# Slot order for tokens of x, u and the output, stores in two halves, and a new order, in a gated-attention and token-mixing kernel

## The chip, the cores and the metric

The kernel runs on one core of a Trainium2 chip. The metric is the device time of one execution in microseconds. A core has five engines with a queue of their own: TensorE (PE, matmuls; its weight loads are listed as PEld), VectorE (DVE), ScalarE (ACT), GpSimd (POOL) and SyncE (SP, which here only issues transfers). Transfers between HBM and the on-chip memory run on 16 DMA engines; here SP and ACT issue them.

## The reference, cut to what matters

Four sequences of 768 tokens with 8 heads of 48 go through a linear attention with a decay per token and key dimension. The result, 384 wide, is x of a mixer: one pair of products over the tokens, one over the channels.

```python
for t in range(S):
    state = alpha[:, :, t, :, None] * state + np.einsum('bhd,bhe->bhde', k[:, :, t], v[:, :, t])
    y[:, :, t] = np.einsum('bhd,bhde->bhe', q[:, :, t], state)
...
h = np.maximum(xt @ w_tok1, 0.0) @ w_tok2      # over the 768 tokens, 256 wide
u = x + h.transpose(0, 2, 1)
h2 = np.maximum(u @ w_ch1, 0.0) @ w_ch2        # over the 384 channels, 1536 wide
return (u + h2)
```

All inputs and the output are float32. The kernel computes in bf16 with float32 sums.

## The kernel before, in words

**Chunks.** A batch of 768 tokens is cut into 3 chunks of 256, 12 chunks in all, called n = 0 to 11. A load brings one of alpha, k, q, v of a chunk as a tile of 128 partitions, 384 KB: partition p holds the tokens 2p and 2p + 1, its two *slots* (line 541, `load`). For chunk n the operations are: logarithms of alpha (`ln`, `lnP`), their running sum on PE (`cum`), its exponentials on ACT (`E`, `IE`), the products of k and q with them (`kk`, `kl`, `qq`, `ql`, line 653), a transposition of both, the products G of keys and queries (`G0_`, `G1_`, one for each half of 128 tokens), a mask (`mask0_`, `mask1_`, line 720, on DVE), the states K, `s`, `sa`, `sm`, the result `y`, and its copy to a tile of x (`x0_`, `x1_`, 128 tokens each).

**Transposition.** For the chunks 0 to 5 it runs on PE (`trk`, `trq`, line 666) and the result is copied from PSUM (`evk`, `evq`). For the chunks 6 to 11 it is a DMA transpose that SP issues (`dk`, `dq`, line 677), and the query gets one copy more (`pq`). The key's columns are in slot order after it. The query's copy (`qev`) also puts the two slots of each token next to each other, so that x, and with it u and the output, have their tokens in order on the partitions. For the chunks from 3 on, some halves of the keys are copied to the other partitions (`ka`, `kb`, `kc`); `kc` writes over the tile that `dk` reads, and so waits for it, and K waits for `kc`.

**Mixer.** For each batch b: `t1_b` (x by the first token weight, line 805), `ht`, `t2_b` (by the second, line 810), `u` (line 814), the transposition of u (on PE for the batches 0 and 1, `up` and `ut`; by DMA for 2 and 3, `ux`), `c1_b` (line 829, 24 groups of 3 matmuls), `rt` (the maximum with 0, on ACT line 800 or DVE line 802), `c2_b` (line 834), the output's addition `o` (line 838, DVE) and its store `st` (line 585). The last tile of the last batch is cut into 320 and 64 columns (`h0`, `h1`). There are four tiles for o and 20 load tiles. The weights come in 16 pieces of 384 KB (`ldw`) and are cast to bf16 (`cw`, line 698).

**Order.** Every operation, its engine and its place is written out in a list (`ORDER`: the last letter is the engine, t for PE, s for ACT, v for DVE, g for POOL, y for SP), with the buffer numbers of the tiles in another (`BUFS`). Engines take their operations strictly in that order. A planner made the lists beforehand; it is not part of the program. `f` are filler matmuls while PE waits. In the built program transfers take turns on eight semaphores, over both queues, so a transfer waits until the eighth before it has landed.

**Constants.** `mk` (the mask) is made by two fills and two selections on POOL (lines 512 to 516) and a copy on DVE (line 530).

Of the kernel before, what the change touches and what calls it, by code (L numbers as in the profile page):

```python
# [116 lines left out]
def build(g):  # L117
# [12 lines left out]
    def attention(n):  # L130
# [56 lines left out]
        if n < NX:  # L187
            bk, bq = V("one"), V("one")
            trk = O("trk", pe([128] * 8), 8, writes=[bk], reads=[pkk], preds=kk + fill("trk", bk),
                    emit=lambda e: g.trw(bk, pkk, True))  # L190
# [3 lines left out]
                    emit=lambda e: g.trw(bq, pkq, False))  # L194
            evq = O("evq", either(dve(1024 * 1.065), act(1024 * 1.34)), 9, writes=[tpq], reads=[bq], preds=[trq],
                    emit=lambda e: g.qev(e, tpq, g.bank(bq).bitcast(BF16)))
        else:
# [5 lines left out]
            evq = O("pq", either(dve(1024), act(1024 * 1.35, True), {"POOL": (1100.0, 1140.0)}), 9.5, port=True, writes=[tpq], reads=[tqx], preds=[xq],  # L203
# [72 lines left out]
    def weight(nm, piece, prio, work=1100.0):  # L276
        raw = V("in")
        o = P.op(f"ldw_{nm}{piece}", {"SP": (420.0, 420.0), "ACT": (374.0, 374.0)}, prio, writes=[raw],
                 emit=lambda e: g.weight(e, nm, piece, raw, o), dma=("i", work, 1500.0, 650.0))
        wl[(nm, piece)] = P.op(f"cw_{nm}{piece}", either(dve(768, True), pool_cp(768), act(768, True)), prio + 1,  # L280
                               reads=[raw], preds=[o], port=True, emit=lambda e: g.wcast(e, nm, piece, raw))

    def mixer(b):
# [56 lines left out]
        for i in range(NS):  # L340
            hold = 4000.0 if (i >= NS - 3 and b < B - 1) else 0.0
            cuts = [(0, 320), (320, HD)] if (b, i) == LAST else [(0, HD)]
            for ci, (ca, cz) in enumerate(cuts):
# [14 lines left out]
                P.op(f"st_{nm}", {"SP": (420.0, 420.0), "ACT": (374.0, 374.0)}, m0 + (16800 + 1950 * (i + 1)) * sc + hold,  # L358
                     reads=[o_], preds=[oo], emit=lambda e, i=i, o_=o_, ca=ca, cz=cz: g.store(e, o_, b, i, ca, cz),
                     dma=("o", OUT_NS * (cz - ca) / HD, 1000.0, 520.0))  # L360
# [15 lines left out]
f1_trq0t f3_cumw0t f3_trk0t ld_at0y ln0s f1_trq1t f3_trq0t ld_at1y ln1s cumw0t Et0s IE0s E0s f3_cumw1t cumw1t E1s  # L376
f3_K0t Et1s ld_kt0y kk0v f1_K0t ld_qt0y qq0v ql0v trq0t ld_vt0y ld_qt1y kl0v trk0t vb0v K0t evq0s IE1s evk0v G0_0t
vs1_0s ld_at2y ln2s s0_0v mask0_0v qq1g ql1g ib0t G1_0t sa1_0t f3_trq1t trq1t evq1s cumw2t E2s ld_kt1y kl1v IE2s
sm1_0v kk1g trk1t mask1_0v y1_0t x1_0s ld_vt1y Et2s vb1g K1t vs1_1g sa0_1t evk1v G0_1t ld_kt2y kk2v f1_G11t G1_1t kl2v
trk2t evk2s sm0_1v sa1_1t ld_qt2y ql2g ld_vt2y vb2s mask1_1v ib1t y1_1t x1_1s sm1_1v qq2g ia1t trq2t evq2s K2t sa0_2t  # L380
mask0_1v vs0_0g y0_0t x0_0v ld_at3y P3g lnP3s f3_G12t ln13s G0_2t ldw_wt10y cw_wt10g vs0_1g G1_2t t1_0_1_0t t1_0_1_1t
y0_1t x0_1s sm0_2v t1_0_0_0t mask0_2v cum3t E3s t1_0_0_1t t1_0_0_2t IE3s t1_0_1_2t ldw_wt11y cw_wt11g t1_0_0_3t ia2t
vs0_2g y0_2t x0_2s vs1_2g ib2t mask1_2v y1_2t x1_2s t1_0_1_3t t1_0_1_4t ld_kt3y kk3v k0a3v kl3v t1_0_0_4t ldw_wt21y
cw_wt21s t1_0_0_5t ht_0_0v t1_0_1_5t ht_0_1s ldw_wt20y cw_wt20g ka3g trk3t evk3v t2_0_3t u_0_3v t2_0_0t u_0_0v t2_0_2t
ld_at4y P4g t2_0_4t ln14s u_0_2v t2_0_1t u_0_1v lnP4s t2_0_5t u_0_5v up_0_1t ut_0_1s up_0_0t cum4t r13s E4s r14s kb3g
ldw_wc11y u_0_4v up_0_2t cw_wc11g ut_0_0v c1_0_2_0t rt_0_2_0s ldw_wc10y ld_vt3y ldw_wc13y IE4s cw_wc10v c1_0_0_0t
ut_0_2v c1_0_3_1t c1_0_1_1t kc3v vb3v c1_0_3_0t rt_0_3_1v ld_qt3y vs1_3v qq3v rt_0_1_1v q0r3v ql3v ldw_wc14y cw_wc13s
c1_0_7_0t c1_0_0_1t vs0_3s rt_0_3_0s rt_0_0_0s cw_wc14s c1_0_1_0t ldw_wc15y cw_wc15g rt_0_1_0v rt_0_7_0v K3t c1_0_6_1t
rt_0_0_1s trq3t rt_0_6_1v evq3s s0_3v c1_0_8_0t rt_0_8_0s sa1_3v ld_qt4y c1_0_8_1t rt_0_8_1v c1_0_7_1t rt_0_7_1s
c1_0_6_0t G1_3t mask1_3v G0_3t qq4g ldw_wc12y q0r4g ql4g c1_0_10_0t rt_0_10_0v c1_0_10_1t rt_0_10_1v c1_0_11_0t  # L390
cw_wc12s c1_0_4_1t trq4t c1_0_2_1t ld_kt4y rt_0_6_0v evq4s c1_0_5_0t mask0_3v c1_0_9_1t ldw_wc21y c1_0_5_1t c1_0_4_0t
cw_wc21s rt_0_4_0s rt_0_11_0v ib3t kk4g ld_qt5y k0a4g y1_3t kl4g kb4g rt_0_4_1v ld_at5y ln15s c1_0_11_1t rt_0_5_0v
ldw_wc20y c1_0_9_0t rt_0_9_1v trk4t rt_0_2_1s x1_3v y0_3t P5g lnP5s rt_0_11_1v rt_0_9_0s cw_wc20g c2_0_0_0t rt_0_5_1s
cum5t ldw_wc22y evk4v G0_4t ld_vt4y G1_4t mask1_4v sm1_3g x0_3s cw_wc22g c2_0_4_0t mask0_4v r15s q0r5g c2_0_0_1t
c2_0_4_1t vb4s vs1_4g vs0_4s ka4s kc4g E5s qq5v c2_0_1_0t ia4t ldw_wc23y cw_wc23s ldw_wc24y cw_wc24v c2_0_2_0t
c2_0_2_1t K4t sa0_4v IE5s c2_0_1_1t c2_0_1_2t c2_0_2_2t c2_0_4_2t ldw_wc25y y0_4t sm0_4v sa1_4v ld_at6y ib4t cw_wc25s
c2_0_1_3t P6v lnP6s y1_4t x1_4s trq5t ld_kt5y k0a5v kk5v c2_0_4_3t o_0_4v x0_4s ld_at7y sm1_4g ld_vt5y P7g ld_kt6y
cum6t evq5s trk5t evk5v ln16s c2_0_0_2t c2_0_0_3t vb5s vs0_5g vs1_5s ln17s r17s E6s o_0_1v G0_5t r16s mask0_5v G1_5t
mask1_5v c2_0_5_0t c2_0_5_1t c2_0_5_2t c2_0_5_3t ia5t y0_5t ld_at8y kc5g K5t P8v t1_1_1_0t t1_1_1_1t sa0_5v x0_5s
t1_1_1_2t t1_1_1_3t t1_1_1_4t c2_0_2_3t sm0_5v ib5t y1_5t o_0_5v x1_5s k0a6g t1_1_0_0t t1_1_0_1t IE6s kk6v t1_1_0_2t  # L400
kb6v t1_1_0_3t t1_1_0_4t ld_qt6y ld_qt7y t1_1_0_5t ht_1_0s t1_1_1_5t ht_1_1s c2_0_3_0t c2_0_3_1t t2_1_3t t2_1_1t
u_1_3v u_1_1v ld_vt6y t2_1_0t vb6s u_1_0v vs1_6g lnP7s st_0_5s lnP8s t2_1_2t ka6g u_1_2v cum7t t2_1_5t u_1_5v cum8t
st_0_1y E7s t2_1_4t u_1_4v c2_0_3_2t IE7s ld_at10y o_0_2v up_1_0t ut_1_0s ld_vt7y up_1_1t ut_1_1v ld_kt7y q0r6g
ld_at9y o_0_0v up_1_2t dk6y ut_1_2s qq6g dq6y vb7g c2_0_3_3t o_0_3v k0a7v kk7v IE8s vs0_6s E8s kc6s c1_1_2_0t
c1_1_6_0t rt_1_6_0s vs1_7s c1_1_11_1t c1_1_1_0t rt_1_1_0v q0r7g ld_qt8y c1_1_4_0t rt_1_11_1v ld_kt8y c1_1_8_0t
c1_1_5_0t dk7y c1_1_0_1t rt_1_4_0v rt_1_5_0s qq7v dq7y K6t rt_1_0_1s c1_1_0_0t c1_1_11_0t ln19s kb7s P9g ld_kt9y
rt_1_2_0v ka7s vs0_7g ln18s lnP9s rt_1_8_0s P10g lnP10s ld_vt8y c1_1_7_0t rt_1_0_0v c1_1_3_0t s0_6v sa1_6v rt_1_7_0v
sm1_6g k0a8v c1_1_6_1t c1_1_8_1t r18s q0r8v c1_1_10_0t c1_1_3_1t rt_1_11_0s kc7g c1_1_9_1t c1_1_4_1t rt_1_8_1v ld_qt9y
rt_1_10_0s rt_1_3_0s c1_1_7_1t rt_1_3_1s rt_1_7_1s K7t cum9t c1_1_1_1t rt_1_4_1s kk8v sa0_7v sm0_7v st_0_2s c1_1_9_0t
c2_1_1_0t st_0_4s IE9s rt_1_9_1s E9s rt_1_1_1s c1_1_2_1t ln110s r19s c1_1_5_1t sa1_7v pq6g G0_6t pq7s rt_1_6_1v  # L410
rt_1_9_0v dk8y qq8v dq8y st_0_0s G1_6t c2_1_1_1t c2_1_1_2t c1_1_10_1t c2_1_1_3t ld_qt10y rt_1_2_1s c2_1_4_0t rt_1_5_1v
# [12 lines left out]
rt_2_8_1s c1_2_0_0t c1_2_2_0t c1_2_9_1t rt_2_2_0v st_1_1s rt_2_0_1s rt_2_9_1s c1_2_1_0t K10t sa0_10v sm0_10v c2_2_5_0t
# [468 lines left out]
```

## Time and profile before

| | |
|---|---|
| time, median of 3 runs | 164.9 us (163.66 to 165.65) |
| time of the profiled execution | 164.64 us |
| its span | 162.9 us |
| PE busy | 154.4 us (95%) |
| DVE, ACT, POOL busy | 119.7, 94.8, 66.7 us |
| moved by DMA | 34.46 MB, of it 25.17 MB read from HBM and 4.72 MB written |
| granted PE clock | 1.00 until the end |

The span runs from the first to the last instruction; the time has some 1.7 us around it. A busy matmul counts until its modelled end, so in a row of matmuls of 326 ns each the next one starts 162 ns after the one before. In the rows, "ps" is PSUM, L834 is line 834, and what stands behind an arrow in brackets is what ended the idle time before the row.

### The profile page before, as it was taken

The page shows a single profiled execution, that of the slowest core. Times are in us where ns is not written, and L with a number is a line of the kernel's source. Part 1 is how long each engine was busy: PE and PEld are TensorE (multiplying, and loading weights), DVE is VectorE, ACT ScalarE, POOL GpSimd, SP SyncE. Part 2 cuts the span into 40 slices and gives each one's busy share as a digit, 9 for nine tenths or more (in the row PEclk, how much of TensorE's full clock was granted, in tenths as well). Part 3 has the DMA queues.
Part 4 walks back from the last instruction along what each step waited for, and adds up shares of the span by engine and source line. Part 5 has one row for each costly group of instructions (what it writes and reads, how often), then busy time and mean ns, then how long its engine had stood idle before and what let it go on. Part 6 is the DMA issues. An engine that isn't in the chain of part 4 may idle for free.

```text
span 162.9 us, 4036 instructions
## 1 busy us (share of the span) xinstructions
PE 154.4 (95%) x1598; PEld 97.8 (60%) x1598; DVE 119.7 (73%) x214; ACT 94.8 (58%) x178; POOL 66.7 (41%) x87
## 2 busy tenths in 40 slices
PE   7989798999999999989899999999999999999992
PEld 2556564566676766645567766666666656666661
DVE  4188988999979996996799888878788345442231
ACT  3878686796597787749996873248941211435000
POOL 4045694509982333938159999352130000000000
PEclk9999999999999999999999999999999999999998
DMA  5999999999899998999999999998511067200115
GB/s 130 325 325 322 281 352 347 315 329 336 278 346 269 274 324 203 320 121 269 242 277 175 239 258 187 165 275 233 117 48 50 2 129 209 97 4 0 48 60 181
DMA packets 76322, 34.46 MB, mean 212 GB/s; under 512 B 68112, under 2 KB 76304, under 8 KB 76304
## 3 DMA queue, kind: packets, MB, share of 16 engines
q1 hardware_dynamic: 74000, 31.10, 75.5%
q10 hardware_dynamic: 2304, 3.11, 5.2%
q8 instruction: 12, 0.20, 0.5%
q14 instruction: 6, 0.05, 0.1%
HBM read 25.17 MB, written 4.72 MB: 183 GB/s over the span
## 4 chain that ended last, share of the span: by engine, by line
PE 75%; DMA 12%; ACT 4%; DVE 2%; SPq 2%; issue 1%; POOL 1%; POOLq 0%; DVEq 0%; ACTq 0%
PE ps L834 29%; PE ps L829 24%; PE ps L604 13%; DMA tpk<-pkk 5%; DMA in<-in_moe_w_tok_dram 4%; PE ps L810 4%; PE ps L805 4%; DMA in<-in_alpha_dram 3%; SPq L545 2%; ACT rt L800 2%; PE ps L666 1%; DVE pkq L653 1%; POOL pkq L653 1%; DVE wc L698 1%; POOL wt L698 1%
## 5 line engine op out<-in xcount | busy, mean ns | idle before, releaser
L834 PE MATMUL ps<-wc,rt 128*128 128x384 bf16 (+2 forms) x300 | 52.9, 320 | 0.0
L829 PE MATMUL ps<-ut,wc 128*128 128x384 bf16 x288 | 50.2, 326 | 0.6 <-ACT rt L800 0.5
L829 PEld LDWEIGHTS <-wc 128*128 128x128 bf16 x288 | 27.3, 98 | 18.8 <-issue 0.9
L834 PEld LDWEIGHTS <-rt 128*128 128x128 bf16 x300 | 27.2, 98 | 16.4
L800 ACT ACTIVATE rt<-ps 128x384 bf16<-128x384 f32 x53 | 23.8, 490 | 19.9 <-PE ps L829 19.6
L720 DVE TENSOR_TENSOR gtm<-ps,mk 128x1024 bf16<-128x1024 f32 x24 | 28.7, 1218 | 3.0 <-PE ps L604 2.7
L802 DVE TENSOR_SCALAR rt<-ps 128x384 bf16<-128x384 f32 x43 | 22.5, 551 | 7.3 <-PE ps L829 7.2
L838 DVE TENSOR_TENSOR o<-ps,u 128x384 f32<-128x384 f32 (+2 forms) x25 | 13.2, 539 | 12.8 <-PE ps L834 9.6
L653 POOL TENSOR_TENSOR pkq<-in,E 128x384 bf16<-128x384 f32 (+1 forms) x9 | 11.4, 1272 | 9.3 <-DMA in<-in_q_dram 7.7
L814 DVE TENSOR_TENSOR u<-ps,x 128x384 bf16<-128x384 f32 x24 | 11.9, 550 | 3.4 <-PE ps L810 3.4
L653 DVE TENSOR_TENSOR pkk<-in,IE 128x384 bf16<-128x384 f32 (+1 forms) x11 | 7.6, 703 | 6.4 <-ACT IE L637 4.0
L697 ACT CAST x<-ps 128x384 bf16<-128x384 f32 x16 | 7.5, 481 | 7.3 <-PE ps L604 7.2
L698 POOL CAST vb<-in 64x384 bf16<-64x384 f32 (+1 forms) x17 | 9.4, 558 | 4.4 <-ACT vb L697 2.2
L805 PE MATMUL ps<-x,wt 128*128 128x384 bf16 x48 | 10.8, 325 | 0.0
L697 ACT CAST vb<-in 64x384 bf16<-64x384 f32 (+1 forms) x16 | 10.4, 653 | 0.3
L697 ACT COPY tpq<-ps 128x1024 bf16<-128x1024 bf16 x6 | 7.9, 1321 | 4.5 <-PE ps L666 4.5
L810 PE MATMUL ps<-ht,wt 128*128 128x384 bf16 x48 | 9.4, 326 | 0.5 <-POOL wt L698 0.5
L604 PE MATMUL ps<-zs 128*128 128x512 bf16 x25 | 8.3, 472 | 1.5 <-DVE zs L507 1.1
L604 PE MATMUL ps<-vb,gtm 128*128 128x48 bf16 x192 | 8.5, 183 | 0.7 <-DVE gtm L720 0.6
L653 POOL TENSOR_TENSOR pkk<-in,IE 128x384 bf16<-128x384 f32 (+1 forms) x6 | 8.5, 1409 | 1.4 <-DVE pkk L653 1.1
L604 PEld LDWEIGHTS <-gtm 128*128 128x128 bf16 x192 | 7.3, 96 | 2.2 <-DVE gtm L720 1.0
L604 PE MATMUL ps<-tpq,tpk 48*64 48x128 bf16 (+1 forms) x288 | 8.1, 219 | 0.6 <-ACT tpq L697 0.5
(93 smaller groups left out, 211.0 us busy)
## 6 DMA issues: line engine op xcount, KB each, us to landing
in<-in_alpha_dram SPq DMA_DIRECT2D x12, 384.0 KB, 5.6
in<-in_k_dram SPq DMA_DIRECT2D x12, 384.0 KB, 4.9
in<-in_q_dram SPq DMA_DIRECT2D x12, 384.0 KB, 5.2
in<-in_v_dram SPq DMA_DIRECT2D x12, 384.0 KB, 4.9
in<-in_moe_w_ch_dram SPq DMA_DIRECT2D x12, 384.0 KB, 6.3
out_dram<-o ACTq DMA_DIRECT2D x15, 192.0 KB, 1.9
in<-in_moe_w_tok_dram SPq DMA_DIRECT2D x4, 384.0 KB, 5.5
out_dram<-o SPq DMA_DIRECT2D x8, 192.0 KB, 2.7
```

The lines of the kernel that those rows point to most:

```text
L604: return self.pe.matmul(out, lhsT=lhsT, rhs=rhs, start=start, stop=stop, skip_group_check=True)
L653: self.shared(self.eng[e].tensor_tensor(self.t(dst)[:, c : c + z, :, 0:D], self.t(src)[:, :, c : c + z, :].rearrange("p h s d -> p s h d") ...
L697: return self.act.copy(d, s)
L698: return self.shared(self.eng[e].tensor_copy(d, s))
L720: self.nc.vector.tensor_tensor(self.t(gtm)[:, hf, :, :], self.pair(gp).rearrange("p a (j t) -> p (a j) t", t=128), bass.AP(tensor=m.tensor ...
L800: self.act.activation(d, s, AF.Relu)
L802: self.nc.vector.tensor_scalar_max(d, s, 0.0)
L805: self.pe.matmul(self.bank(bank)[:, 0:HD], lhsT=self.wt1[:, kc, m * 128 : m * 128 + 128], rhs=self.t(x), start=(kc == 0), stop=(kc == NS - 1))
L810: self.pe.matmul(self.bank(bank)[:, 0:HD], lhsT=self.wt2[:, kc, i * 128 : i * 128 + 128], rhs=self.t(hts[kc]), start=(kc == 0), stop=(kc = ...
L829: self.pe.matmul(self.bank(bank)[:, 0:HD], lhsT=self.wc1[:, kc, mc * 128 : mc * 128 + 128], rhs=self.t(ut)[:, 3 * half : 3 * half + 3, kc, ...
L834: self.pe.matmul(self.bank(bank)[:, 0 : cz - ca], lhsT=self.t(rts[mc][0])[:, i * 128 : i * 128 + 128], rhs=self.wc2[:, mc, ca:cz], start=( ...
L838: self.nc.vector.tensor_tensor(self.t(o)[:, ca:cz], self.bank(bank)[:, 0 : cz - ca], self.t(u)[:, i % 3, ca:cz], ALU.add)
```

## The change

Five things are changed.

1. Tokens of x, u and the output stay in slot order: partition 64 s + t of a tile holds token 2t + s of its 128. The copies of the query from PSUM (`evq`) are then plain copies, written like those of the key; the transposition of the query on PE writes the same layout as the key's. The copy `pq` moves runs of 64.
2. The rows of the first token weight are loaded in the same order: each of its two pieces comes in two transfers of 64 partitions (`ldw_wt10a`, `ldw_wt10b`, ...). The columns of the second are permuted in its cast, which reads its f32 tile with a step of two.
3. Each store becomes two: partitions 0 to 63 to the even rows, 64 to 127 to the odd rows (`st_...a`, `st_...b`). 25 stores become 50; 33 of them are issued by ACT (16 before), 17 by SP (9 before).
4. The mask is put together by four copies on DVE from `u2` and `us`, two constants that are there already; POOL's four operations for it go.
5. `ORDER` and `BUFS` are made anew: for all engines the operations stand in another order, and some are on another engine. For instance kc6 moves from ACT to POOL. The same 1,598 matmuls are issued.

```diff
@@ attention
-            evq = O("evq", either(dve(1024 * 1.065), act(1024 * 1.34)), 9, writes=[tpq], reads=[bq], preds=[trq],
-                    emit=lambda e: g.qev(e, tpq, g.bank(bq).bitcast(BF16)))
+            evq = O("evq", either(dve(1024, True), act(1024)), 9, writes=[tpq], reads=[bq], preds=[trq],
+                    emit=lambda e: g.trwev(e, tpq, bq))
@@ mixer
-                P.op(f"st_{nm}", {"SP": (420.0, 420.0), "ACT": (374.0, 374.0)}, m0 + (16800 + 1950 * (i + 1)) * sc + hold,
...
+                for slot in range(2):
+                    P.op(f"st_{nm}" + "ab"[slot], {"SP": (420.0, 420.0), "ACT": (374.0, 374.0)},
...
@@ constants
-        gp.memset(self.mk, 1.0)
-        gp.memset(mkb, 1.0)
-        for t, base in ((self.mk, 0), (mkb, 127)):
-            gp.affine_select(out=t, in_=t, compare_op=ALU.is_ge, fill=0.0, base=base,
-                             pattern=[[1, 128]], channel_multiplier=-2)
...
-        dv.tensor_copy(self.mk[64:128], mkb[64:128])
+        dv.tensor_copy(self.mk[0:64, 0:64], self.u2[0:64, 0:64])
+        dv.tensor_copy(self.mk[0:64, 64:128], self.u2[0:64, 0:64])
+        dv.tensor_copy(self.mk[64:128, 0:64], self.us[64:128, 64:128])
+        dv.tensor_copy(self.mk[64:128, 64:128], self.u2[64:128, 64:128])
@@ weight
-            w = self.w[0].rearrange("(c p) m -> p c m", p=128)
-            self.gated(dma(t.rearrange("p (c m) -> p c m", c=3), w[:, 3 * piece : 3 * piece + 3, :]), op)
+            w = self.w[0].rearrange("(c p s) m -> s p c m", p=64, s=2)[slot]
+            self.gated(dma(t[64 * slot : 64 * slot + 64].rearrange("p (c m) -> p c m", c=3),
+                           w[:, 3 * piece : 3 * piece + 3, :]), op)
@@ wcast
-            d, t = self.wt2[:, :, 384 * piece : 384 * piece + 384], t.rearrange("p (c m) -> p c m", c=2)
+            d = self.wt2[:, :, 384 * piece : 384 * piece + 384].rearrange("p c (i s t) -> p c i s t", s=2, t=64)
+            t = t.rearrange("p (c i t s) -> p c i s t", c=2, s=2, t=64)
@@ store
-        self.queue(e).dma_start(self.out[b, i * 128 : (i + 1) * 128, ca:cz], self.t(o)[:, ca:cz])
+        self.queue(e).dma_start(self.out[b, i * 128 : (i + 1) * 128, ca:cz].rearrange("(t s) c -> s t c", s=2)[slot],
+                                self.t(o)[64 * slot : 64 * slot + 64, ca:cz])
@@ trw
-            self.pe.transpose(k[:, c % 4, :, c // 4, :] if keys else o[:, c * 128 : c * 128 + 128],
+            self.pe.transpose(k[:, c % 4, :, c // 4, :],
@@ qev
-        self.copy(e, self.t(d).rearrange("p (j c s) -> p s j c", j=4, s=2),
-                  s.rearrange("p (s j c) -> p s j c", s=2, j=4))
+        self.copy(e, self.t(d).rearrange("p (g s t) -> p s g t", s=2, t=64),
+                  s.rearrange("p (s g t) -> p s g t", s=2, t=64))
@@ ORDER (around the first DMA transpose)
-ld_at9y o_0_0v up_1_2t dk6y ut_1_2s qq6g dq6y vb7g c2_0_3_3t o_0_3v k0a7v kk7v IE8s vs0_6s E8s kc6s c1_1_2_0t
+up_1_0t u_1_3v up_1_1t dk6y t2_1_4t kc6g ln18s E7s ld_vt7y st_0_0by P9g st_0_0ay c2_0_5_3t kb6s ut_1_1v t2_1_5t
```

More of the change, by code (lines that the diff above doesn't have):

```diff
@@ L202, in attention @@
                    emit=lambda e: g.xbar(tqx, pkq), dma=("x", 1400.0, 1180.0, 480.0))
-            evq = O("pq", either(dve(1024), act(1024 * 1.35, True), {"POOL": (1100.0, 1140.0)}), 9.5, port=True, writes=[tpq], reads=[tqx], preds=[xq],
+            evq = O("pq", either(dve(1024, True), act(1024, True), {"POOL": (1100.0, 1140.0)}), 9.5, port=True, writes=[tpq], reads=[tqx], preds=[xq],
                     emit=lambda e: g.qev(e, tpq, g.t(tqx)))
@@ L277, in weight @@
         raw = V("in")
-        o = P.op(f"ldw_{nm}{piece}", {"SP": (420.0, 420.0), "ACT": (374.0, 374.0)}, prio, writes=[raw],
-                 emit=lambda e: g.weight(e, nm, piece, raw, o), dma=("i", work, 1500.0, 650.0))
+        los = []
+        for slot in range(2 if nm == "wt1" else 1):
+            o = P.op(f"ldw_{nm}{piece}" + "ab"[slot] * (nm == "wt1"), {"SP": (420.0, 420.0), "ACT": (374.0, 374.0)}, prio,
+                     writes=[raw], emit=lambda e, slot=slot: g.weight(e, nm, piece, raw, los[slot], slot),
+                     dma=("i", work / (2 if nm == "wt1" else 1), 1500.0, 650.0))
+            los.append(o)
         wl[(nm, piece)] = P.op(f"cw_{nm}{piece}", either(dve(768, True), pool_cp(768), act(768, True)), prio + 1,
-                               reads=[raw], preds=[o], port=True, emit=lambda e: g.wcast(e, nm, piece, raw))
+                               reads=[raw], preds=los, port=True, emit=lambda e: g.wcast(e, nm, piece, raw))
     def mixer(b):
@@ L505, in __init__ @@
         self.mk = T([128, 128], BF16, "mk")
-        mkb = self.T["rt"][0][:, 0:128]
         dv.memset(self.zs, 0.0)
```

147 lines of the change are left out of this document (75 added, 72 removed), and 22 rows, old and new, of the table BUFS.

## The prediction

> **What bounds the kernel now.** I read the page first, then busy time by stage, then the chain of work that ended last, then the stages where TensorE (PE) is not full.
>
> ```profile
> span 162.9 us, 4036 instructions
> ...
> PE 154.4 (95%) x1598; PEld 97.8 (60%) x1598; DVE 119.7 (73%) x214; ACT 94.8 (58%) x178; POOL 66.7 (41%) x87
> ```
>
> Busy time by stage (columns: stretch, its length, then busy us and instructions of PE, PEld, DVE, ACT, POOL, granted clock, DMA share, GB/s):
>
> ```profile
> 6.40:31.50 25.10, 22.24 (x310) 14.44 (x309) 21.59 (x35) 18.87 (x32) 14.42 (x19) 1.00 1.12 325
> 31.50:60.00 28.50, 28.37 (x301) 18.78 (x302) 26.25 (x44) 22.63 (x42) 15.22 (x19) 1.00 1.04 307
> 60.00:82.00 22.00, 20.68 (x180) 12.85 (x176) 17.88 (x33) 16.97 (x38) 10.36 (x12) 1.00 1.05 237
> 82.00:120.00 38.00, 38.00 (x476) 24.60 (x478) 32.10 (x51) 25.54 (x49) 24.28 (x25) 1.00 0.95 205
> 120.00:159.80 39.80, 39.80 (x329) 24.84 (x321) 19.55 (x35) 7.85 (x17) 0.47 (x1) 1.00 0.24 72
> ```
>
> PE is full except in two stages: the start (2.86 us idle, besides fillers) and 60 to 82 (1.32 us). DVE is nearly full in the second row (26.25 of 28.50), and DMA is busy in every stage up to 120.
>
> The chain:
>
> ```profile
> 1.06 5.35 PE ps L604 x24
> ...
> 19.77 7.10 DMA in<-in_moe_w_tok_dram
> ...
> 27.02 0.84 POOL wt L698
> ...
> 31.36 0.87 DVE wc L698
> ...
> 32.28 3.59 PE ps L829 x21
> ...
> 64.89 7.62 DMA tpk<-pkk
> ...
> 136.38 11.70 PE ps L829 x72
> ...
> 159.91 0.22 DVE o L838
> ```
>
> It runs through PE, save three places: the first loads, the second piece of the second token weight (landed at 26.87, cast until 27.86), and the transpose dk6. 72 matmuls in 11.70 us give a pace of 0.1625 us each, which is the price of a 384-column matmul below. The chain's first c1 pair after all casts stands at 32.28; another ran at 31.51 and then waited 0.29, so c1 starts at 31.8 in effect.
>
> The built programs tell the rest of the frame: both issue the same 1,598 matmuls, and the same set stands ahead of the first c1. So what the change can move is the start of c1, PE's waits behind it, and the tail. (31.8 to the last matmul is 128 us in both, less or more waits.)
>
> **The change part by part.**
>
> *Query copies.* The rows of today's copy, and of the key copy that the new one equals in shape:
>
> ```profile
> L697 ACT COPY tpq<-ps 128x1024 bf16<-128x1024 bf16 x6 | 7.9, 1321 | 4.5 <-PE ps L666 4.5
> L698 DVE COPY tpk<-ps 128x1024 bf16<-128x1024 bf16 x5 | 3.5, 692 | 1.1 <-PE ps L666 1.1
> L697 ACT COPY tpk<-ps 128x1024 bf16<-128x1024 bf16 x1 | 1.0, 1013 | 1.5 <-PE ps L666 1.5
> L697 ACT COPY tpq<-tpk 128x1024 bf16<-128x1024 bf16 x4 | 5.4, 1355 | 0.0
> L698 POOL CAST wt<-in 128x768 bf16<-128x768 f32 x3 | 2.5, 825 | 2.3 <-DMA in<-in_moe_w_tok_dram 2.3
> ```
>
> Six ACT copies (6 x 1.32 = 7.9) become four on ACT (4.05) and two on DVE (1.4). The later six go from four ACT and two POOL to three and three, each between 1.0 (the key copy) and 1.355; I take 1.05, the key copy being nearest, so ACT loses about 6 us of 94.8. PE waits for none of it but at the start, so: 0, bounds -0.6 (two copies of the start, 0.3 each) and 0.
>
> *Mask built from u2 and us.* Four POOL operations and one DVE copy become four small DVE copies ahead of the first load's landing: 0 on the path; bounds -0.2 and +0.2, as DVE's first product waits for ACT until 7.3.
>
> *wt1 in four half transfers, wt2 cast with a step of two.* Bytes are the same. The cast reads f32 with a step of two; no row has that. The nearest strided copy is today's query copy, 0.31 over the straight one, so 0 to +0.31 for cw_wt21, which is on the path; I take +0.1, because here the step is on the read side. The Trainium skill (SBUF — State Buffer, "Door 1: The DMA port swizzle") says a step is free while neighbours share a 16-byte line, up to 4 f32 or 8 bf16: by it this cast costs 0. The trace disagrees for a written step of two bf16 (1321 against 1013 ns), so I do not lean on it; by the page the forecast would be 0.1 less.
>
> *25 stores become 50.* The rows of the output tile, the full queues, and the transposes' landing:
>
> ```profile
> L585 ACTq DMA_DIRECT2D out_dram<-o x16: 338/338/444, 63.3 to 160.0; - x16
> ...
>   DVE o L838: 3.0, 2
> ...
> DMA to landing us min/median/max: 1.8/2.0/5.2
> ```
>
> ```profile
> DMA to landing us min/median/max: 3.1/4.5/7.6
> ```
>
> ACT issues 33 instead of 16 (17 x 0.34 = 5.8 us, which eats what the copies freed), SP 17 instead of 9. Bytes and row lengths stay. Two couplings come with it. An output tile (of four) is free only when both halves landed, and DVE already waited 3.0 us for that twice. And the built program lets each transfer wait for the landing of the eighth before it, on either queue, so twice the stores means that loads, transposes and stores wait on nearer ones. They are priced under the order.
>
> *The order, start.* One load takes SP
>
> ```profile
> 3.06 1.15 SPq L545 DMA_DIRECT2D in<-in_q_dram  x1
> ...
> 12.74 1.15 SPq L545 DMA_DIRECT2D in<-in_v_dram  x1
> ```
>
> (12.74 - 3.06) / 8 = 1.21 us per load. Before, t2 needs the 18th load (26.87 + cast, 27.86), with five of its six pairs behind it, ending 29.7. After, three pairs need only the piece that stands 15.5 loads deep (some 3 us earlier) and three need the 18th. What then ends last is attention: DVE from kt2's landing (10th load in both) to the last mask has 6 short operations at 0.49 and 4 masks at 1.22 = 7.8 us, from 16.7, so 24.5; before it ends at 24.70:
>
> ```profile
> 22.35 2.35 DVE L720 TENSOR_TENSOR gtm<-ps,mk 128x1024 bf16<-128x1024 f32 x2
> ```
>
> Then x, t1's last, ht: t2 starts at 26.7, three pairs run to 27.7, the cast of the 18th ends at 27.7, and t2 ends at 28.8 instead of 29.7. The same u, transposes and copies follow. c1 at 31.1 instead of 31.8: -0.7; bounds -1.3 (18th load without its queue lag) and +0.8 (DVE's chain slips by a mask, less the gain).
>
> *The order, 31 to 64.* DVE from the first state of chunk 3 to the second ht of batch 1 has 38 operations (6 masks, 3 wide products at 0.95, two copies 0.69, a cast, 26 at 0.5 to 0.55): 25.4 to 26.6 us, where PE's own list takes 25.2. So 0.2 to 1.4 late, I take 0.7. Before, the same sum over its list gives 0.5. Net +0.2.
>
> *The order, transposes.* Before, PE's waits in 60 to 82 are these, and ACT's in front of them:
>
> ```profile
> 73.16 0.34 PE L604 MATMUL ps<-vb,pkk 128*128 128x96 bf16 x4 [0.44 <-ACT pkk L697]
> 73.67 0.33 PE L604 MATMUL ps<-vb,kt 128*128 128x96 bf16 x4 [0.17 <-ACT rt L800]
> ...
> 77.89 2.11 PE L829 MATMUL ps<-ut,wc 128*128 128x384 bf16 x12 [0.48 <-ACT rt L800]
> 80.23 0.33 PE L604 MATMUL ps<-vb,pkk 128*128 128x96 bf16 x4 [0.23 <-ACT rt L800]
> ```
>
> ```profile
> 72.59 0.51 ACT L697 COPY pkk<-pkk 64x384 bf16<-64x384 bf16 x1 [2.04 <-DMA tpk<-pkk]
> ```
>
> ACT stood 2.04 us for dk6, with the rt copies queued behind. With 0.16 of pipeline each the four waits cost 1.32 + 0.64 = 2.0 us. After, kc6 is on POOL, so ACT's rt no longer wait behind it. But K6 stands 37.8 us of PE work behind c1's start (40.2 before), so PE wants it at 31.1 + 37.8 + 0.7 = 69.6. And dk6's eighth transfer before is now st_0_1a, on ACT at about 61.2, with SP's later loads queued behind dk6. The store lands after 2.0 to 5.2 us in full queues, I take 4.1, nearer the maximum, as the DMA share is 1.05 in that stage: 65.3. dk6 lands 4.5 later (3.1 to 7.6), 69.8, kc6 0.5: K6 at 70.3 to 70.4, PE waits 0.8. Then three ACT stores at 75 to 77 wait for transfers (qt9, at10, st_0_2b) that SP issues behind dk6; they come within 1 us of it, +0.6. In all 1.4 instead of 2.0: -0.6. Bounds: -2.0 (no wait at all) and +3.0 (store 5.2, dk6 7.6, so K6 at 74.5).
>
> *The order, 82 to 120.* Three output additions (o_1_0, o_1_2, o_2_5) now stand 2 to 4 us behind a half store of their tile on ACT; with 2.0 to 5.2 to landing DVE waits up to 3.2 us, as in the row above, and there it cost PE nothing (38.00 of 38.00). +0.4; bounds 0 and +1.5.
>
> *Tail.* After the last addition two halves are issued per queue instead of one:
>
> ```profile
> 160.16 0.33 SPq L585 DMA_DIRECT2D out_dram<-o  x1
> ```
>
> The last addition but one ends 0.13 us ahead of that issue, so the first of each queue goes at about 160.02 on this scale and the second 0.38 later (0.34 and a gap of 0.04), at 160.40: +0.24. SP has two halves more just ahead: +0.4, bounds 0.2 and 0.7. The halves land no earlier for being smaller:
>
> ```profile
> out_dram<-o ACTq DMA_DIRECT2D x15, 192.0 KB, 1.9
> ...
> out_dram<-o SPq DMA_DIRECT2D x1, 32.0 KB, 1.8
> ```
>
> *Sum.* -0.7 + 0.2 - 0.6 + 0.4 + 0.4 + 0.1 = -0.2. The profiled execution took 164.64 us (span 162.9, 1.74 around it), the median of the three runs is 164.9. Forecast: 164.4.
>
> **The rivals.**
>
> *Faster.* DVE's chain and dk6 come in time: start -1.3, transposes -2.0 (K6 leaves ACT's queue), late 0, tail +0.2: -3.1, so 161.5. For it: the 6 us that ACT's copies free, and that kc6 moves to POOL, which is busy for 10.36 of 22 us there. Against it: DVE's sum (0.7 late) does not depend on either.
>
> *Slower: dk6 behind the doubled stores.* If dk6 lands later than 71.6 on this scale, K6's wait passes 2.6 and eats the start's gain; from there each us of landing is a us of the end. At the rows' worst (store 5.2, dk6 7.6) K6 is at 74.5, and the ACT stores at 75 to 77 stand in front of rt for about as long: the sum is -0.2 + 3.6 + 0.4, 168.4; the middle of this case is 167. For it: the DMA share of 1.05 in this stage, and that before dk6 itself took 7.6. Against it: SP stands at dk6, so the queues drain and it should land nearer to 4.5. The Trainium skill (DMA: Bandwidth & Descriptors, "Rules for kernel authors") says not to cut a transfer into two partition halves, since both spread over the same 16 engines and run one after the other; by that rule the split buys nothing here and this case is what is left of it. The trace agrees in the last rows above (1.9 and 1.8 us, whatever the size); how long the waits behind it get it does not show.
>
> *The copies are not cheaper.* If the new query copies keep 1.32, the start loses two times 0.3: 165.0. That lies within the forecast's own range.
>
> **How the numbers follow.** The forecast (near no change, its own range 163.2 to 166.2) 0.40, with the third rival in it; faster 0.26; slower 0.34, since every edit but the order adds waits and DVE has no room. Low: 162.2, between the faster case and the forecast; high: 168.0, near the slow case's end; about 1 in 10 is left out on each side. A run of this kernel tells some 1% (1.6 us) from no change, so the chances of faster by over 1%, within, slower are 0.26, 0.40, 0.34.
>
> **What would show it.** Start: the first c1 matmul near 31.1, t2 not waiting for the last cast of wt. Copies: tpq near 1013 on ACT and 692 on DVE. 31 to 64: ht of batch 1 waits for DVE. K6: PE idle of about 0.8 us, released by POOL's pkk, near 70. Late: DVE's o waiting for out_dram more than 3.0 us, PE full. Tail: 0.4 us more between the last matmul and the end. It is wrong if PE idles over 2 us between 60 and 82, if ACT's stores show waits ahead of rt, or if c1 starts after 32.

## The result, and the profile after

The changed kernel takes 169.5 us (median of 6 runs, 169.28 to 170.62), the kernel before beside it 164.7 (163.66 to 165.65): a ratio of 1.031, interval 1.027 to 1.035, so 4.8 us slower. The forecast was 164.4, its range 162.2 to 168.0. Medians here are of all runs; the ratios, here and below, leave out single runs that were slow (over 1.5% above the fastest of their kernel). The profiled execution took 170.6 us, one more than the median; what is read from the trace below adds up to its time. Its page:

```profile
span 168.6 us, 4088 instructions
...
PE 155.0 (92%) x1598; PEld 98.5 (58%) x1598; DVE 118.3 (70%) x218; ACT 93.2 (55%) x179; POOL 66.5 (39%) x81
```

PE issues the same 1,598 matmuls (155.0 us busy, 154.4 before), and DVE, ACT and POOL have a little less work than before. Busy time by stage, with the columns of the table shown for the kernel before (the last two rows are cut at this kernel's last matmul):

```profile
6.40:31.50 25.10, 21.23 (x308) 14.35 (x307) 19.26 (x31) 18.03 (x31) 13.47 (x16) 1.00 1.13 300
31.50:60.00 28.50, 28.02 (x300) 18.26 (x297) 24.48 (x43) 22.67 (x45) 15.30 (x21) 1.00 1.04 306
60.00:82.00 22.00, 21.94 (x190) 14.07 (x187) 17.81 (x34) 16.22 (x36) 16.29 (x18) 1.00 1.09 249
82.00:120.00 38.00, 35.10 (x447) 22.88 (x446) 31.82 (x51) 22.10 (x44) 18.93 (x18) 1.00 1.04 215
120.00:163.50 43.50, 43.28 (x352) 26.88 (x351) 21.92 (x40) 11.22 (x24) 1.33 (x2) 1.00 0.28 63
163.50:168.60 5.10, 0.04 (x2) 0.00 (x0) 0.87 (x3) 0.00 (x0) 0.00 (x0) 0.84 0.44 106
```

Read the first number after the comma. From 60 to 82, where PE idled for 1.32 us, it is now full (21.94 of 22.00). But the start has 1.0 us more idle PE, 82 to 120 has 2.90 us where there was none, and the last row is 5 us in which only transfers run.

From the trace I take three lengths: the start of the first c1 matmul, from there to the end of the last matmul, and from there to the landing of the last store. Before: 31.51, 128.30 and 2.17, together 161.98. After: 32.35, 131.19 and 3.96, together 167.50. So of 5.5 us in the two profiled executions the start has 0.8, the waits between 2.9, the tail 1.8. The first c1 matmuls, before and after:

```profile
31.51 2.73 PE L829 MATMUL ps<-ut,wc 128*128 128x384 bf16 x14
...
32.35 1.95 PE L837 MATMUL ps<-ut,wc 128*128 128x384 bf16 x11
```

**Start.** The chain of waits of the changed kernel:

```profile
19.33 6.30 DMA in<-in_moe_w_tok_dram
...
25.69 1.64 POOL wt L706 x2
27.32 0.96 POOL in L653
...
28.31 0.56 DVE pkk L661
```

The last half of the first token weight landed at 25.63. POOL casts it, then the first piece of the second, and only then makes the product of chunk 3 that pkk and, in DVE's queue, u wait for. Less moves meanwhile. The stretch from 18 to 26 us (last column GB/s), before:

```profile
18.00:26.00 8.00, 7.29 (x116) 4.79 (x113) 7.33 (x11) 6.71 (x12) 6.34 (x9) 1.00 1.06 322
```

and after, where the DMA share is even higher (1.16), 278:

```profile
18.00:26.00 8.00, 6.92 (x126) 5.08 (x123) 7.81 (x12) 6.21 (x10) 3.14 (x5) 1.00 1.16 278
```

By the landings in the trace, the four halves came 1.16, 0.95, 0.95 and 1.00 us behind the load ahead of them; a whole load of twice the bytes took 1.0 to 1.4 in the same stretch before (but for one of 2.59).

**Stores.** The output tiles' transfers (issue min/median/max in ns), and who waited for them:

```profile
L592 ACTq DMA_DIRECT2D out_dram<-o x33: 472/495/837, 61.4 to 164.8; - x33
L592 SPq DMA_DIRECT2D out_dram<-o x17: 466/560/1342, 63.7 to 165.7; - x17
...
  DVE o L846: 4.4, 2
...
DMA to landing us min/median/max: 1.8/2.2/4.7
```

Half a store holds its queue for longer (0.47 at least) than a whole one did (0.34). All 25 stores took 11.0 us of issue, the 50 take 27.9, ACT's own 17.9 instead of 5.6. On DVE, the longest wait:

```profile
119.14 0.56 DVE L846 TENSOR_TENSOR o<-ps,u 128x384 f32<-128x384 f32 x1 [2.42 <-DMA out_dram<-o]
119.62 0.55 DVE L810 TENSOR_SCALAR rt<-ps 128x384 bf16<-128x384 f32 x1
```

and what it does to PE:

```profile
120.22 0.97 PE L837 MATMUL ps<-ut,wc 128*128 128x384 bf16 x5 [1.82 <-DVE rt L810]
```

This addition is o_1_2. Its sums were ready at 107.81, but its tile is free only when both halves of o_1_3 have landed. st_1_3b landed at 117.14; st_1_3a was issued on ACT at 114.94, behind rt and vb, and landed at 119.05. Behind o_1_2 in DVE's queue stands the rt that makes room for c1_2_6_0: PE waits 1.99 us (1.82 idle in the row, and the 0.16 by which the next matmul otherwise starts before the one ahead of it ends; PE's waits below are counted in this way too).

**Tail.** The last additions wait for tiles too, and then SP has four halves to issue, 2.60 us of them:

```profile
163.09 1.41 DVE L846 TENSOR_TENSOR o<-ps,u 128x384 f32<-128x384 f32 x3 [1.96 <-DMA out_dram<-o]
163.68 2.60 SPq L592 DMA_DIRECT2D out_dram<-o  x4
```

From the last matmul to the end of the last addition: 0.96 us (0.32 before); to the last issue 1.23 more (0.03 before); to landing 1.77 (1.82 before).

### The profile page after: what moved, and what is told of

Its sections match the earlier page's. It is cut to its first block, busy times and chain, and to the rows that moved or that the text cites. A ratio compares the mean times of both kernels' runs of the same rounds, so it can differ in the third digit from the quotient of the medians.

```text
span 168.6 us, 4088 instructions
## 1 busy us (share of the span) xinstructions
PE 155.0 (92%) x1598; PEld 98.5 (58%) x1598; DVE 118.3 (70%) x218; ACT 93.2 (55%) x179; POOL 66.5 (39%) x81
## 4 chain that ended last, share of the span: by engine, by line
PE 50%; DMA 17%; DVE 9%; POOL 9%; SPq 4%; ACT 3%; issue 3%; ACTq 1%; DVEq 0%; POOLq 0%
PE ps L837 21%; PE ps L842 13%; PE ps L612 9%; DMA out_dram<-o 4%; DMA tpk<-pkq 4%; DMA in<-in_moe_w_tok_dram 4%; PE ps L818 4%; DMA in<-in_v_dram 3%; DMA in<-in_q_dram 3%; PE ps L813 2%; SPq L550 2%; POOL wc L706 1%; SPq L566 1%; DVE pkk L661 1%; POOL in L653 1%
## 5 line engine op out<-in xcount | busy, mean ns | idle before, releaser
L837 PE MATMUL ps<-ut,wc 128*128 128x384 bf16 x288 | 51.1, 326 | 1.8 <-DVE rt L810 1.8
L808 ACT ACTIVATE rt<-ps 128x384 bf16<-128x384 f32 x56 | 25.3, 489 | 31.1 <-PE ps L837 30.2
L810 DVE TENSOR_SCALAR rt<-ps 128x384 bf16<-128x384 f32 x40 | 21.1, 550 | 12.0 <-PE ps L837 11.9
L706 POOL CAST vb<-in 64x384 bf16<-64x384 f32 (+1 forms) x14 | 8.3, 593 | 13.3 <-DMA in<-in_v_dram 4.9
L705 ACT CAST vb<-in 64x384 bf16<-64x384 f32 (+1 forms) x19 | 12.0, 631 | 2.5 <-DMA in<-in_v_dram 1.7
L779 POOL TENSOR_TENSOR ss<-tmp,E 128x384 bf16<-128x384 f32 x7 | 5.8, 833 | 14.2 <-DVE tmp L776 8.2
L813 PE MATMUL ps<-x,wt 128*128 128x384 bf16 x48 | 10.3, 326 | 0.3 <-POOL wt L706 0.3
```

What stands on the lines that cost most here:

```text
L705: return self.act.copy(d, s)
L808: self.act.activation(d, s, AF.Relu)
L810: self.nc.vector.tensor_scalar_max(d, s, 0.0)
L813: self.pe.matmul(self.bank(bank)[:, 0:HD], lhsT=self.wt1[:, kc, m * 128 : m * 128 + 128], rhs=self.t(x), start=(kc == 0), stop=(kc == NS - 1))
L837: self.pe.matmul(self.bank(bank)[:, 0:HD], lhsT=self.wc1[:, kc, mc * 128 : mc * 128 + 128], rhs=self.t(ut)[:, 3 * half : 3 * half + 3, kc, ...
```

## The experiments

Theory H: the halves cost the time, those of the weight at the start, those of the stores in DVE's waits and the tail. Rival O: the new order does, by what it puts behind what. The code below is shortened to what differs.

**e1 and e4: stores of 128 partitions with rows in their places.**

```diff
-  dma_start(out_rows.rearrange("(t s) c -> s t c", s=2)[slot], o[64 * slot : 64 * slot + 64])
+  dma_start(out_rows.rearrange("(t s) c -> s t c", s=2), o)
```

> The changed kernel with each output tile stored by one transfer again (128 partitions, rows in the same places), which stands where the first of its two halves stood. Theory H (the halves cost the time): in the changed kernel's profile the tail from the last matmul to the last landing took 3.96 us against 2.17 before, and c1_2_6_0 waited 1.99 us behind output additions whose tiles wait for halves still to be stored. Both should go: 169.5 - 1.8 - 2.0 = 165.7 us, with the last landing 2.2 us behind the last matmul. Theory O (the new order itself holds PE up, whatever the stores look like): only the second issue of each queue in the tail goes, at most 0.6 us, so 169 us, and PE waits some 2 us before c1_2_6_0 as it did.

> Slot order with plain query copies, the mask by DVE copies and the second token weight cast with a step, but the order of before and no transfer halved (stores of 128 partitions with rows in their places; the first token weight in token order, so the token products are made with permuted rows). What is left of the change is the copies and the stepped cast. Both theories: the copies are hidden, 164.4 to 164.8 us; 164.1 if the two copies of the start count 0.3 each, 165.1 if the stepped cast costs 0.3.

Measured: 220.4 us (ratio 1.335, 1.326 to 1.343) and 221.0 (1.328, 1.316 to 1.340). Neither theory foresaw that. In e1's page DVE stands still for tiles:

```profile
L844 DVE TENSOR_TENSOR o<-ps,u 128x384 f32<-128x384 f32 (+2 forms) x25 | 13.0, 535 | 39.4 <-DMA out_dram<-o 31.8
```

Each of e1's stores took 6.4 to 15.0 us to land and left three completions in the trace, where a store of the other runs has sixteen. The Trainium skill (DMA: Bandwidth & Descriptors, "Rules for kernel authors") says that an outermost dimension of fewer than 16 confines a transfer to that many engines; here it is two. The trace agrees in kind, with fewer completions and late landings; how many engines worked is in no view here. So the layout has no such cheap way out, and these runs tell nothing on H and O. The later kernels store whole tiles in neighbouring rows instead.

**e2, e5, e6, e12: the new order without one or both kinds of halves.** Each half transfer becomes a whole one at the place of the first of its two:

```diff
-  ldw_wt11by ... ldw_wt11ay          (e2, e6, e12)
+  ldw_wt11y
-  st_1_3bs ... st_1_3as              (e5, e6, e12)
+  st_1_3s
```

> The changed kernel with the two pieces of the first token weight loaded by one transfer each, at the place of their first halves. The rows of that weight are then in token order, so the token products are made with permuted rows; every instruction but the four transfers is the same. Theory H: in the changed kernel's start, halves landed 0.9 to 1.05 us apart, nearly as far as whole loads (1.0 to 1.6), so two transfers fewer bring the 18th load some 1.9 us forward and c1 from 32.35 to about 31.1: 168.3 us. Theory O: c1 starts late because POOL's casts of the weights stand in front of the products of chunk 3, which stays: c1 at 32.2, 169.4 us.

> The changed kernel with each output tile stored by one transfer of 128 neighbouring rows, as before, where the first of its two halves stood; the output's rows are then out of order within each 128. The wt1 pieces stay in halves. Theory H (the halves cost the time): tail from 3.96 back to 2.2 us, -1.8; the waits of 1.99 us before c1_2_6_0 and part of the 1.23 before G0_9 go, -2.0: 165.7 us. Theory O (the new order holds PE up): only the tail's second issues, -0.6: 168.9 us, with about 2 us of idle PE before c1_2_6_0.

> The changed kernel with no halves at all: one store for each tile (rows out of order within each 128) and one transfer for each piece of the first token weight (token order, so the token products are made with permuted rows), each at the place of its first half. What is left are the plain copies, the stepped cast and the new order. Theory H: the 4.8 us are gone, 164.0 to 164.8. Theory O: 167 us or more, since whole wt1 pieces alone gave 167.7 and the waits of 120 remain.

> The kernel of e6 once more, whose four times lay between 165.07 and 167.93, to tell what the new order costs without any halves. Order harmless: 165.0 to 165.5, as e7. Order costs some 2 us of its own: 167.4, with PE's wait in front of G0_9 or c1_2_6_0 longer than in e6's profile (0.27 and 1.02).

**e3, e7, e8, e11: the order of before with both, none, or one kind of halves,** one behind the other on the same queue:

```diff
-  st_1_3y
+  st_1_3ay st_1_3by                  (e3, e8)
-  ldw_wt10y
+  ldw_wt10ay ldw_wt10by              (e3, e11)
```

> The changed kernel with the order and the buffers of the kernel before; both halves of a store or of a piece of the first token weight stand where the one transfer stood, on the same queue. Theory H: start +0.6 to +1.9 (two more transfers ahead of the 18th load), tail +1.4, some waits for output tiles: 167.5 to 168.5 us. Theory O: the halves cost only the tail's second issue, 165.2 us, and the rest of the loss of 4.8 us is the order's.

> The same with the order and buffers of before: only the plain copies, the mask by DVE and the stepped cast are left of the change. Both theories: hidden copies, 164.4 to 164.8 us; down to 164.1 if the start's two copies count 0.3 each, up to 165.1 if the stepped cast does.

> The order of before, each store in two halves one behind the other on the queue of the one store, first token weight in whole pieces (token order, so the token products are made with permuted rows). Theory H: of the 4.8 us that both kinds of halves cost in this order about 2.5 to 3 stay: 167.2 to 167.7, with a tail of 3.5 us or more behind the last matmul. Theory O (stores hardly matter): 165.5.

> The order of before, first token weight in halves, each tile stored by one transfer (rows out of order within each 128). Theory H with its parts adding up: c1 starts at 32.5 as in e3 (31.66 without halves in e7), nothing else: 165.0 + 0.85 = 165.9 us, tail 2.2. Rival: the halves of the weight shift all later transfers, and e3's waits of 3.6 us between c1 and the last matmul come with them: 168 us.

Measured, as ratios to the kernel before with their intervals:

| halves | new order | order of before |
|---|---|---|
| none | 1.000 (0.996 to 1.005), e12 | 1.002 (0.998 to 1.006), e7 |
| weight | 1.012 (1.003 to 1.021), e5 | 1.004 (1.000 to 1.009), e11 |
| stores | 1.015 (1.007 to 1.022), e2 | 1.022 (1.015 to 1.030), e8 |
| both | 1.031 (1.027 to 1.035), the change | 1.028 (1.018 to 1.037), e3 |

e6, the same kernel as e12, gave 1.010 (1.000 to 1.020) in four runs between 165.07 and 167.93 us; e12's twelve lay between 164.15 and 167.09. The table's entry is that of the longer series.

In the order of before the table settles H against O: without halves it takes the time of the kernel before, with both kinds it loses some 3%. In the new order that holds by e12 alone: by e6 the order itself would cost 1.0%, the weight's halves 0.2% more, the stores' 0.4% and both kinds 2.0%. Differences of the table's entries, of 164.7 us: the stores' halves cost 2.0 to 2.3% (3.3 to 3.8 us) in the order of before and 1.5 to 1.9% (2.4 to 3.1) in the new one; the weight's 0.2 to 0.5% (0.4 to 0.9) and 1.2 to 1.6% (1.9 to 2.6). By the intervals, each of these may be off by some 1%. From the traces (us; the profile of e2 is not read, since that execution took 171.52 us and the other three 167.24 to 168.02):

| | first c1 | to the last matmul | tail |
|---|---|---|---|
| before | 31.51 | 128.30 | 2.17 |
| e7, order of before, no halves | 31.66 | 128.29 | 2.19 |
| e11, weight | 32.80 | 127.96 | 2.20 |
| e8, stores | 31.61 | 128.92 | 4.08 |
| e3, both | 32.49 | 131.91 | 4.11 |
| e6 and e12, new order, no halves | 31.21, 31.14 | 128.92, 129.76 | 2.23, 2.23 |
| e5, weight | 32.91 | 130.12 | 2.24 |
| after, both | 32.35 | 131.19 | 3.96 |

The first and the last column follow the halves and nothing else: the weight's put c1 off by 0.8 to 1.2 us in the order of before and by 1.1 to 1.8 in the new one, the stores' add 1.7 to 1.9 us of tail. The middle column moves by 0.8 us between two profiles of one kernel (e6, e12), so its tenths mean little. E3's 131.91 is more than e8 and e11 explain together; its profiled execution was a long one (171.41 us; two others took 169.43 and 169.93), and the rest stays open.

e5 (167.6) lies between H's 165.7 and O's 168.9: its tail is short, as H had it, but PE still waits 1.45 us in front of G0_9 and 0.91 in front of c1_2_6_0. That second wait is again o_1_2's, whose tile now waits for a whole store. It stands in all three kernels of the new order with whole stores; in e12:

```profile
116.50 0.56 DVE L842 TENSOR_TENSOR o<-ps,u 128x384 f32<-128x384 f32 x1 [0.90 <-DMA out_dram<-o]
...
117.57 0.65 PE L833 MATMUL ps<-ut,wc 128*128 128x384 bf16 x3 [0.30 <-DVE rt L806]
```

**e9: no output addition waits for a tile.**

```diff
 def t(self, v):
+    if v.cls == "o" and v.buf > 3:       # o_1_2 and later: load tiles no longer used
+        return self.T["in"][...][:, 0:HD]
```

> The changed kernel, but from o_1_2 on each output tile lies in a load tile that is used no more, so that no output addition waits for an earlier tile's halves to land. All transfers and places are the same. Theory T (the halves cost time because a tile is free only when its second half has landed): in the changed kernel's trace o_1_2 began at 119.14, when tile 3 came free at 119.05, though its sums were ready at 107.81; o_2_5 waited from 118.39 to 120.80, o_3_1 from 161.97 to 162.90. Without that c1_2_6_0 waits only the 1.0 us for the transposed u that e5 and e6 showed, -1.0, and the last additions come 0.9 earlier: 167.6 us. Rival Q (the queues' issues set the time, tiles do not): the tail stays near 4 us behind the last matmul, 168.6 to 169.5.

Measured: 167.7 us (1.013, 1.006 to 1.021) instead of 169.5, as theory T had it (167.6). o_1_2 runs at once, without idle time before it:

```profile
116.36 0.55 DVE L849 TENSOR_TENSOR in<-ps,u 128x384 f32<-128x384 f32 x1
```

PE no longer waits in front of c1_2_6_0, the middle is 129.11, and the tail 3.12. So held tiles cost this kernel 1.8 us by the medians, 2.9 by the ratios and by the lengths in the two traces. Not all of it is the halves' doing: with whole stores o_1_2 waits 0.90 us (e12), 1.34 (e5) and 1.57 (e6) for its tile, against 2.42, and PE 0.46 to 1.02 in front of c1_2_6_0, against 1.99. The expectation put e5's and e6's wait there down to the transposed u; in the traces that had landed over 6 us earlier, and DVE's rt ended the wait. The tail's 0.9 us over 2.2 are still there with no addition waiting for a tile, so they belong to the halves' own issues and landings (the last issue takes 0.75 us in e9, 0.38 in e12).

**e10 and e13: the kernel before with its stores in halves, by rows or by columns.**

```diff
-  dma_start(out_rows[:, ca:cz], o[:, ca:cz])
+  dma_start(out_rows[64 * slot : 64 * slot + 64, ca:cz], o[64 * slot : 64 * slot + 64, ca:cz])   (e10)
+  dma_start(out_rows[:, half], o[:, half])                                                       (e13)
```

> The kernel before with each store in two halves one behind the other on its queue, each of 64 partitions to 64 neighbouring rows. The output is the reference's. In e8, where the halves go to every other row, one issue took 0.47 to 0.76 us instead of 0.34, and the last landing came 4.1 us behind the last matmul. Theory R (the step between rows makes the issue dear): issues of 0.34 again, tail 2.2 + 0.4 = 2.6 us, 165.2 us. Rival N (it is the number of transfers and the 64 partitions): tail near 4 us and 167.5 us or more, as in e8.

> The kernel before with each store in two halves, one behind the other on its queue, cut by columns: 128 partitions and 192 columns each. As many transfers as in e10 (168.2 us, tail 4.1, issues of 0.47 and 0.60). Theory P (64 partitions make an issue dear): issues of 0.34, tail 2.2 + 0.4 = 2.6 us, 165.6 us or a little more. Rival N (the second of two transfers makes it dear): issues of 0.47 to 0.60 and 168 us.

Measured: 168.2 us (1.018, 1.012 to 1.024) and 167.7 (1.015, 1.006 to 1.023), tails of 4.09 and 2.85. The issues of e10:

```profile
L589 ACTq DMA_DIRECT2D out_dram<-o x32: 473/604/1107, 63.6 to 162.7; - x32
L589 SPq DMA_DIRECT2D out_dram<-o x18: 466/591/1464, 58.2 to 162.9; - x18
```

and of e13, with as many transfers of as many bytes:

```profile
L589 ACTq DMA_DIRECT2D out_dram<-o x32: 338/424/1547, 64.8 to 163.0; - x32
L589 SPq DMA_DIRECT2D out_dram<-o x18: 332/432/3088, 59.1 to 163.2; - x18
```

The step between rows is not the price: theory R of e10 falls, its issues are those of e8. An issue is dear because it covers 64 partitions (0.47, and 0.60 right behind another), not because there are two: with 128 partitions the first mostly takes 0.33 to 0.34 and the second 0.39 to 0.47. Nor is it the length of the rows, since a whole store has rows as long as e10's and takes 0.34. The shorter issues of e13 take 1.2 us out of the tail. The whole time hardly shows it; e13's middle was 130.47 in its profile, and its interval overlaps e10's. So twice the transfers cost something even with 128 partitions; where, these runs do not say.

**e14: the weight's pieces in two transfers of 128 partitions.**

```diff
-  w = w1.rearrange("(c p s) m -> s p c m", p=64, s=2)[slot]     # 64 partitions, 3 blocks
+  w = w1.rearrange("(c p) m -> p c m", p=128)                   # 128 partitions, 2 blocks or 1
```

> The changed kernel with each piece of the first token weight still in two transfers at the same places, but each of 128 partitions: one of 256 KB, one of 128 KB, rows of 1 KB as before (token order, so the token products are made with permuted rows). Theory P (64 partitions move slower): the four land in 2/3 and 1/3 of a whole load's time, the 18th load comes 1.5 us earlier and c1 starts near 31.3: 168.0 us. Rival N (any transfer takes its 0.9 us however small): c1 at 32.3, 169.5 us.

Measured: 168.3 us (1.022, 1.014 to 1.030), c1 at 31.31, as theory P had it (168.0, 31.3). The transfers landed 0.75, 0.72, 0.34 and 0.38 us behind the load ahead of them, so by their bytes, and the stretch from 18 to 26 moves as much as before:

```profile
18.00:26.00 8.00, 6.96 (x119) 5.13 (x120) 7.62 (x10) 6.11 (x10) 5.44 (x7) 1.00 1.09 320
```

Four transfers instead of two cost at most 0.2 us of c1 here (31.31; 31.14 and 31.21 in e12 and e6); four of 64 partitions cost 1.0 or more. The halves of 64 partitions also read every other row of the weight, and no run separates the two for a load.

**e15: the new order with the old layout, dq9 issued earlier.**

```diff
-  dk9y ... ld_kt10y dq9y
+  dk9y ... dq9y ld_kt10y        (in the kernel before, with the new order and whole transfers)
```

> The kernel before (tokens in order, strided query copies, whole transfers) with the order and buffers of the changed kernel, whole transfers at the place of their first halves, and on SP the transpose dq9 issued ahead of the load ld_kt10 instead of behind it. The output is the reference's. In e12's profile (the new order with plain copies) PE waited 1.68 us in front of G0_9 for the copy behind dq9, which landed at 98.05, 7.16 us after its issue. If that wait is what eats the order's gains: c1 at 31.2 to 31.8, no wait at G0_9, 163.5 to 164.2 us, ahead of both kernels. If the waits only move on (c1_2_6_0 for the transposed u, 0.5 to 1.0): 164.6 to 165.4.

Measured: 167.6 us (1.015, 1.010 to 1.021), worse than both expectations. The wait in question, in e12, on ACT and PE:

```profile
98.07 1.05 ACT L701 COPY tpq<-tpk 128x1024 bf16<-128x1024 bf16 x1 [1.71 <-DMA tpk<-pkq]
...
99.17 0.64 PE L608 MATMUL ps<-tpq,tpk 48*64 48x128 bf16 x32 [1.52 <-ACT tpq L701]
```

It is gone in e15 (dq9 lands 3.3 us after its issue instead of 7.2), but PE now waits 0.67 us in front of cum11 and 1.28 in front of c1_2_10_1, for an rt that stands in DVE's queue behind a product waiting 1.70 us for POOL, and c1 starts at 32.59 instead of 31.14. The start's loss of 1.45 is in e15's early copies:

```profile
L697 DVE COPY tpq<-ps 128x1024 bf16<-128x1024 bf16 x2 | 2.6, 1304 | 0.5 <-PE ps L665 0.5
```

The first sums of chunk 0 end 0.55 us later than in e12; e7, which has the new mask too, shows the same delay there, so that part is neither the copies' nor the mask's. Then evq0 on DVE takes 1.30 instead of 0.68 and the two others on ACT 1.30 instead of 1.01, and the lag grows to 1.47 at G0_2. So in this order some 0.9 us of the start hang on the plain copies. In the order of before none does (e7: c1 at 31.66; 31.51 before). That these parts make up all of e15's 2.5 us over e12 isn't shown.

No kernel here beats the one before.

## Why the prediction was wrong, point by point

**The frame was right**: start, waits and tail add up to the loss (0.8 + 2.9 + 1.8 = 5.5 in the profiled executions). The forecast had -0.7 for the start (and +0.1 for the cast), 0.0 for the waits (0.2 - 0.6 + 0.4) and +0.4 for the tail.

**wt1 in halves: "Bytes are the same."** This step failed: it put the cutting of the weight at nothing. Bytes did not set the time. e14 (31.31) and e5 (32.91) show that the halves of 64 partitions, with the step between rows that goes with them, are worth 1.0 to 1.8 us of c1 in the new order. Without it the start came out as worked out: 31.1 predicted, 31.14, 31.21 and 31.31 in e12, e6 and e14. With it, 32.35, and the price of -0.7 became +0.55 on the scale of 31.8; the prediction's own sign, c1 after 32, came true. The wt2 cast with its step took 0.90 us on ACT instead of 0.84: +0.06, near the +0.1; the Trainium skill's rule there (SBUF — State Buffer, "Door 1: The DMA port swizzle") gives 0, which the trace nearly bears out.

**"17 x 0.34 = 5.8 us".** This failed too: the price of an issue was taken from the row of the whole stores. ACT's issues went from 5.6 to 17.9 us, +12.3. The row bounded nothing, since no transfer of 64 partitions stood in that profile; an upper end was missing. The 5.8 us were no term of the sum, and what the dearer issues cost is shown for the tail alone (1.2 us between e10 and e13).

**Tail: +0.4, bounds 0.2 and 0.7.** It was +1.8, outside the bounds: issues of 0.47 to 0.76 in a row on SP, and additions waiting for tiles (o_3_1 from 161.97 to 163.09).

**82 to 120: +0.4, bounds 0 and 1.5.** It was 2.90 us of idle PE, the largest miss of the sum. The mechanism was right for one of the three additions: o_1_2 waited 2.42 us for a half store of its tile; o_2_5 came to a free tile (120.80; it ran at 121.61), and o_1_0 stopped nothing. The size was not. The forecast let PE be full, as in the row of before, but here an rt stood behind o_1_2 in DVE's queue, and PE waited 1.99 us, of which 0.46 to 1.02 stay with whole stores. The forecast asked what DVE waits for and not who waits for DVE. The other wait of that stage, 1.23 in front of G0_9 for the copy pq9, belongs to the order (without halved stores it is 1.45 in e5, 1.68 in e12 and 0.27 in e6) and was in no step.

**Transposes: -0.6.** K6 did not wait at all: 21.94 of 22.00 busy, so the whole 2.0 us went, the lower bound. The rival "dk6 behind the doubled stores" was wrong in its place: "slower" came true by other mechanisms. The Trainium skill's rule beside that rival (DMA: Bandwidth & Descriptors, "Rules for kernel authors": don't cut a transfer into partition halves) was right, and too mild: it says that halves gain nothing, and here both kinds together cost 2 to 3%.

**31 to 64: +0.2.** 0.35 us more idle PE in that row, the longest wait 0.52 before trk5: about right.

**Query copies: 0.** Their durations came as forecast, on ACT and DVE from PSUM and on ACT and POOL behind the DMA transposes (predicted 1013, 692, 1050 and 1050 ns):

```profile
L705 ACT COPY tpq<-ps 128x1024 bf16<-128x1024 bf16 x4 | 4.0, 1010 | 2.5 <-PE ps L674 2.5
...
L706 DVE COPY tpq<-ps 128x1024 bf16<-128x1024 bf16 x2 | 1.4, 685 | 0.3 <-PE ps L674 0.3
...
L705 ACT COPY tpq<-tpk 128x1024 bf16<-128x1024 bf16 x3 | 3.1, 1044 | 4.5 <-DMA tpk<-pkq 2.7 <-POOL in L653 1.8
L706 POOL COPY tpq<-tpk 128x1024 bf16<-128x1024 bf16 x3 | 3.1, 1038 | 0.7 <-DVE in L653 0.7
```

Alone, with the mask and the cast, they are worth nothing (e7, 1.002). That the new order's start leans on them shows only in e15.

**The order as a whole** gave back what it gained: c1 0.3 to 0.4 us earlier and no wait at K6, against 1.3 to 2.1 us of waits at G0_9 and, behind o_1_2's tile, in front of c1_2_6_0 (e6, e12).

## What to carry to other kernels

Before a transfer is cut, look for a row of the shape that it will have; when the profile has none, the row of the uncut one does not bound the price from above (0.34 us an issue became 0.47 to 0.60 here). When a layout forces transfers of half the partitions, count each at its own issue and landing, put the halves of one tile next to each other, and give the tile's next user another buffer, since the tile is held by the later half. For each wait added on an engine, look up what stands behind it and which engine needs that.

## What the runs showed of the hardware that was not expected

- A store of 64 partitions held its queue for 0.47 us, and 0.60 right behind another; one of 128 partitions 0.33 to 0.34 (0.39 to 0.47 as a second), from 32 to 192 KB alike. Whether the rows in HBM are neighbours made no difference (e8, e10).
- Loads of 64 partitions and 192 KB landed 0.95 to 1.16 us (after) and 0.78 to 1.19 (e5) behind the load ahead of them among whole loads, and 0.78 to 0.86 in a row (e3); 256 KB on 128 partitions took 0.72 to 0.75, 128 KB 0.34 to 0.38 (e14). Those of 64 partitions read every other row, those of e14 neighbouring ones.
- A store of 128 partitions whose HBM side is written as two sets of 64 rows took 6.4 to 15.0 us and left three completions instead of sixteen (e1).
